# The second MLP's output product by seven block products, with its x operands stored in DRAM

## Chip, cores and metric

The kernel runs on one core of a Trainium2 chip. The metric is the device time of the program in microseconds (us), median of the runs shown. All matrix work is on TensorE (PE); VectorE (DVE), ScalarE (ACT) and GpSimd (POOL) prepare operands and drain results; every DMA is issued from the queue of SyncE (SP).

## What is computed

With 4 batches of 576 tokens, 8 heads of 64, width DM = 512 and hidden width DF = 1536:

```python
x = attention(q, k, v)                       # windowed, 2304 x 512
xn = x / rms(x) * rms_g                      # first MLP
x = (silu(xn @ w_gate) * (xn @ w_val)) @ w_out
gate = 1 / (1 + exp(-(x @ w_gate2)))         # second MLP, the part that changes
out = (gate * (x @ w_val2)) @ w_out2         # 2304x512 . 512x1536, then 2304x1536 . 1536x512
```

float32 accuracy is kept by splitting each operand into a rounded part (hi, type fp32r) and the rest (lo = value - hi); a product is three matmuls: hi·hi, hi·lo, lo·hi. `split` (L464) makes the two parts: a cast, on ACT or DVE, then a subtraction, on POOL or DVE.

## The kernel before

The work goes through in three stages. Attention and the norm come first, mixed with the first MLP's first pass (passes p = 0 and 1 hold six blocks of 128 hidden columns each, `mlp_step`, matmuls at L1033). The second MLP follows in three passes (p = ONE..LAST) that hold NF = 4 hidden blocks each; a pass goes over the four batches b, forward and backward in turn, and each batch is two units u of two hidden blocks.

`unit` (L1197) computes gate and value for one batch and two hidden blocks. The 2x2 block product (two halves of the width DM, two halves of the 576 tokens) is done by seven block products for eight, with left operands ("11", "12", "22" and the sums S1..S4, made by `weight_blocks`, L535) and right operands ("11", "21", "22" and the differences T1..T4, made by `x_blocks`, L970). One product is six matmuls of 128x128 by 128x288 (L1218). Results collect in three PSUM banks X, Y, Z; X is read out between products by `snap` (ACT, L1228) and `plus` (DVE, L1234), and `finish` applies the gate (ACT tanh, L1244; DVE, L1250) and splits the result into h.

`x_blocks` runs for ten of the twelve (pass, batch) pairs: it loads two tiles `xq` of the first MLP's result from DRAM, makes four differences of 128x576 (L986, or L989 on POOL) and seven splits of 128x576 into the tiles `xo`, `wst`, `xo2`.

The output product is the plain one: `y_group` (L1058, matmuls at L1070) multiplies one hidden block by one block of 128 output columns for 288 tokens, three matmuls of 128x128 by 128x288, and adds up over the four hidden blocks in one of four PSUM banks. Per pass, batch and token half that is 4 x 4 x 3 = 48 matmuls. `late` hands the 32 groups of a batch to the next batch's two units, where they are set between the unit's products; the last batch's are run at the end. `y_evac` (L1136) adds a finished bank to the sums of the passes before (`pt`, L1148; in the first pass a copy, L1141 on DVE or L1143 on ACT), which are kept in DRAM between passes (`o_part`). In the last pass `out_blocks` (L1160) turns a block on DVE and stores it, and `out_rows` (L1175) turns the last token chunk on PE. `weight_late` and `weight_out` prepare the output weights `wo`: twelve splits of 128x512.

The order of instructions on every engine is fixed when the program is built. Each operation is added with its engines, a cost, what it reads and writes and a due time; `Line.emit` is a list scheduler that repeatedly takes, for each engine, the operation that can start first by its own estimates (the due time breaks ties and lets urgent ones pass), and emits it. Tiles come from rings of a fixed number of buffers, so an operation that needs a buffer is placed only when its former user is planned to be done. The numbers in `PARAMS` are due times, penalties for an operation's other engine (`w_hi`, `x_lo`, ...), and release times (`rel2`, `span2`: when the second MLP's weights may be decoded by `words`, L417, and stored by `weight_ahead`, L511). Engines then run their queues in that order, each waiting on semaphores.

## Time and profile before

| | us |
|---|---|
| median of 3 runs | 1047.61 |
| the runs | 1047.01, 1047.61, 1050.1 |
| span of the profiled execution | 1042.3 |
| median less span | 5.3 |

| engine | busy us | share of the span |
|---|---|---|
| PE | 994.6 | 95% |
| DVE | 672.1 | 64% |
| POOL | 539.3 | 52% |
| ACT | 455.0 | 44% |

The profile is of one execution; its span runs from the first to the last instruction, and what lies around the span (5.3 us against the median) is not in it. A matmul is booked with its full latency and overlaps the next, so the pace of PE is read from the distance between starts, not from the booked time. A group's mean time on DVE and POOL contains what the two engines cost each other; the minimum and the median of a view by tile show it without that.

### The profile page before, as it was taken

The numbers are of one execution on the slowest core, as the hardware profiler recorded it, in microseconds if no ns is written. First come the engines' busy times: TensorE is split into PE (matmuls) and PEld (weight loads), VectorE is DVE, ScalarE is ACT, GpSimd is POOL, SyncE is SP. The second block draws the span as 40 slices with busy tenths as digits, with TensorE's granted clock in tenths as the row PEclk, the third lists the DMA queues.
The fourth block names the chain that finished last, engine by engine and source line by source line (L and its number), as shares of the span: only waits on it lengthen the run. The fifth ranks groups of instructions, "written<-read, shape, count | busy, mean of one in ns | idle before, by whom it ended". The sixth has DMA issues, their size and how long they took to land.

```text
span 1042.3 us, 19960 instructions
## 1 busy us (share of the span) xinstructions
PE 994.6 (95%) x7222; PEld 961.2 (92%) x7222; DVE 672.1 (64%) x1431; ACT 455.0 (44%) x1243; POOL 539.3 (52%) x691
## 2 busy tenths in 40 slices
PE   5889789999999999999999999999999999999997
PEld 4667678889999999999999989999999999999996
DVE  4688875676674478778777567456655577465633
ACT  3767646665332442222222454445543355443331
POOL 3467674554453663112114777558655398445510
PEclk9879879999999999999999999999999999999998
DMA  8957646673647565867782331213241433244334
GB/s 182 163 138 179 145 119 169 129 210 111 213 134 260 192 217 183 302 227 233 237 270 94 112 106 56 92 42 128 70 152 50 137 113 129 80 110 119 61 77 92
DMA packets 192978, 152.04 MB, mean 146 GB/s; under 512 B 135760, under 2 KB 164432, under 8 KB 192880
## 3 DMA queue, kind: packets, MB, share of 16 engines
q1 hardware_dynamic: 192880, 150.77, 49.6%
q8 instruction: 57, 0.93, 0.4%
q14 instruction: 41, 0.34, 0.1%
HBM read 103.55 MB, written 47.19 MB: 145 GB/s over the span
## 4 chain that ended last, share of the span: by engine, by line
PE 81%; DVE 7%; POOL 4%; DMA 3%; issue 2%; ACT 2%; SPq 1%; DVEq 0%; POOLq 0%; ACTq 0%
PE y L1070 25%; PE v L1033 14%; PE g L1033 14%; PE att L1218 9%; PE g L1218 6%; PE v L1218 6%; PE att L758 2%; PE att L814 1%; PE att L802 1%; POOL w L470 1%; DMA xo<-in_k_dram 1%; DVE S L545 1%; POOL xo L470 1%; SPq L596 1%; DVE t L1250 1%
## 5 line engine op out<-in xcount | busy, mean ns | idle before, releaser
L1070 PE MATMUL y<-h,wo 128*128 128x288 f32 (+1 forms) x2016 | 367.8, 312 | 0.5 <-POOL h L470 0.5
L1070 PEld LDWEIGHTS y<-h,wo 128*128 128x128 f32 x2016 | 318.6, 188 | 2.0 <-POOL h L470 0.8
L470 POOL TENSOR_TENSOR h<-t,h 128x288 fp32r<-128x288 f32 (+1 forms) x165 | 164.7, 1001 | 279.5 <-ACT h L466 267.4
L1033 PE MATMUL g<-xo,w 128*128 128x384 f32 x864 | 171.1, 346 | 4.8 <-POOL w L470 3.5
L1033 PE MATMUL v<-xo,w 128*128 128x384 f32 x864 | 165.5, 339 | 0.5 <-POOL w L470 0.5
L1033 PEld LDWEIGHTS g<-xo,w 128*128 128x128 f32 x864 | 154.7, 194 | 8.6 <-POOL w L470 4.4
L1033 PEld LDWEIGHTS v<-xo,w 128*128 128x128 f32 x864 | 152.1, 190 | 2.0 <-POOL w L470 1.3
L466 ACT CAST h<-t 128x288 fp32r<-128x288 f32 (+1 forms) x168 | 78.1, 468 | 142.4 <-DVE t L1051 81.0
L1218 PE MATMUL att<-xo,w 128*128 128x288 f32 x576 | 92.2, 295 | 1.3 <-DVE t L1234 1.3
L1045 ACT ACTIVATE t<-g 128x384 f32<-128x384 f32 x72 | 35.4, 492 | 131.2 <-PE g L1033 131.0
L1234 DVE TENSOR_TENSOR t<-t,att 128x288 f32<-128x288 f32 x96 | 43.2, 450 | 71.4 <-PE att L1218 68.0
L1047 DVE SCALAR_TENSOR_TENSOR t<-t,g 128x384 f32<-128x384 f32 x72 | 39.7, 551 | 67.0 <-ACT t L1045 66.9
L1218 PEld LDWEIGHTS att<-xo,w 128*128 128x128 f32 x576 | 81.5, 188 | 1.5 <-DVE t L1234 1.5
L788 POOL TENSOR_SCALAR pr<-pr,rs 128x96 f32<-128x96 f32 x135 | 55.7, 428 | 51.4 <-DVE rs L783 39.0
L470 POOL TENSOR_TENSOR xo<-xq,xo 128x576 fp32r<-128x576 f32 x38 | 58.8, 1555 | 27.5 <-ACT xo L466 22.9
L1218 PE MATMUL v<-xo,w 128*128 128x288 f32 x396 | 63.5, 296 | 1.5 <-DVE t L1234 1.3
L1218 PE MATMUL g<-xo,w 128*128 128x288 f32 x396 | 63.2, 295 | 0.0
L1051 DVE TENSOR_TENSOR t<-t,v 128x384 f32<-128x384 f32 x72 | 39.8, 553 | 34.8 <-PE v L1033 33.8
L456 DVE SCALAR_TENSOR_TENSOR wz<-wst,wz 128x512 int32<-128x512 int32 x72 | 60.9, 848 | 1.4
L459 DVE SCALAR_TENSOR_TENSOR wz<-wst,wz 128x512 int32<-128x512 int32 x72 | 61.0, 850 | 1.1
L453 DVE SCALAR_TENSOR_TENSOR wz<-wst,wz 128x512 int32<-128x512 int32 x72 | 57.1, 793 | 1.6
L1218 PEld LDWEIGHTS v<-xo,w 128*128 128x128 f32 x396 | 55.9, 188 | 2.2 <-DVE t L1234 1.8
(169 smaller groups left out, 1556.2 us busy)
## 6 DMA issues: line engine op xcount, KB each, us to landing
z<-wz SPq DMA_DIRECT2D x54, 256.0 KB
wst<-in_moe_w_gate_dram SPq DMA_DIRECT2D x24, 512.0 KB
wst<-in_moe_w_val_dram SPq DMA_DIRECT2D x24, 512.0 KB
wst<-in_moe_w_out_dram SPq DMA_DIRECT2D x24, 512.0 KB
xq<-y SPq DMA_DIRECT2D x20, 576.0 KB
x<-xo SPq DMA_DIRECT2D x12, 768.0 KB
xo<-x SPq DMA_DIRECT2D x12, 768.0 KB
z<-z SPq DMA_DIRECT2D x36, 256.0 KB
```

Source lines behind the costliest of these rows:

```text
L453: add("DVE", Shared(0.68), lambda: nc.vector.scalar_tensor_tensor(out=z.t, in0=top(), scalar=3, in1=z.t, op0=ALU.logical_shift_left, op1=A ...
L456: add("DVE", Shared(0.68), lambda: nc.vector.scalar_tensor_tensor(out=z.t, in0=top(), scalar=-0x40000000, in1=z.t, op0=ALU.bitwise_and, op ...
L459: add("DVE", Shared(0.68), lambda: nc.vector.scalar_tensor_tensor(out=z.t, in0=low(), scalar=29, in1=z.t, op0=ALU.logical_shift_right, op1 ...
L466: add("ACT", act(n), lambda: nc.scalar.copy(out=hi(), in_=src()), reads=reads, writes=[key] + [order] * bool(order), tiles=tiles + [dst], ...
L470: add("PL", pool(n), lambda: nc.gpsimd.tensor_tensor(out=lo(), in0=src(), in1=hi().bitcast(F32), op=ALU.subtract), reads=reads, writes=[ke ...
L788: add("PL", Shared(0.33), lambda u=u: nc.gpsimd.tensor_scalar(out=pr.t[:, u], in0=pr.t[:, u], scalar1=rs.t[:, u:u + 1], scalar2=1.0, op0=A ...
L1033: nc.tensor.matmul(out=bank.t, lhsT=w[:, l, cols], rhs=x[:, r, j], start=kk == 0 and n == 0, stop=kk == KD - 1 and n == 2)
L1047: add("DVE", dve(T1), lambda: nc.vector.scalar_tensor_tensor(out=t.t, in0=t.t, scalar=1.0, in1=gb.t, op0=ALU.add, op1=ALU.mult), writes=[k ...
L1051: add("DVE", dve(T1), lambda: nc.vector.tensor_tensor(out=t.t, in0=t.t, in1=vb.t, op=ALU.mult), reads=[("bank", p, c, f, 1)], writes=[key] ...
L1070: nc.tensor.matmul(out=yb.t, lhsT=w.t[:, l, s], rhs=h.t[:, r], start=n == 0 and j == 0, stop=n == nf - 1 and j == 2)
L1218: nc.tensor.matmul(out=bank.t, lhsT=l.t[:, a, cols], rhs=r.t[:, d, j], start=first and j == 0 and m == 0, stop=j == 1 and m == 2, skip_gro ...
L1234: add("DVE", dve(T), lambda: nc.vector.tensor_tensor(out=t.t, in0=t.t, in1=bank.t, op=ALU.add), reads=[(key, uk)], writes=[ck[name]], tile ...
```

## The change

The output product of the second MLP is done by seven block products for eight as well. The 2x2 blocks are two hidden blocks of a unit's pair against two halves of 256 output columns (e), and the two token halves. `unit` no longer splits four h tiles; it makes four differences of the gated blocks (`combos`) and seven splits `hop`. `weight_blocks_out` makes seven left operands `wy` out of two `z` tiles, with four sums. `y_products` runs, per pass and batch, 2 x 7 products of six matmuls (two units, three matmuls each), in three of the four PSUM banks y0..y3, and after each product `sum_part` adds the bank to one or two sums; the products are placed in the next batch's units, from slot `y_from` in steps of `y_step` (a slot is one product of the unit).

`x_build` replaces `x_blocks`: it runs once per batch, for batches 0 and 1 during the first MLP's second pass and for 2 and 3 in the second MLP's first pass, and stores each operand in DRAM (`xop_scr`). `x_ops` loads the seven operands where they are used otherwise. The order of the seven products is changed (ORDER, RIGHT, the unit's steps), rings are resized, `out_rows` and `out_blocks` work by halves of the columns, and PARAMS is changed.

```diff
-    "margin": 272.425, "wait": 0.781, "w_sq": 2.027, "w_hi": 0.518, "w_lo": 0.708, "x_hi": 0.345, "x_lo": 0.688,
-    "h_hi": 0.72, "h_lo": 0.667, "qk": 0.226, "norm": 3.767, "pts": 4.555, "o": 0.012, "snap": 38.426, "h_ahead": 56.759, "h2_ahead": 33.839, "evac": 150.0, "holds": (6, 6), "norm_act": 0.994, "slack": 0.0, "share_v": 0.45, "share_p": 0.35, "cold": 1.7, "low": 0.27, "high": 0.38, "recip": 0.43, "rel1": 171.35, "span1": 76.226, "rel2": 360.0, "span2": 192.706, "ys": 1.364,
...
+    "margin": 272.425, "wait": 0.781, "w_sq": 2.027, "w_hi": 0.389, "w_lo": 1.94, "x_hi": 0.358,
+    "x_lo": 0.048, "h_hi": 1.944, "h_lo": 0.349, "qk": 0.226, "norm": 3.767, "pts": 4.555,
+    "o": 0.012, "snap": 53.824, "h_ahead": 56.759, "h2_ahead": 11.517, "evac": 7.152,
+    "rel2": 16.017, "span2": -0.378, "ys": 11.771, "ts": 0.198, "cross": 0.08, "same": 0.064,
+    "exp_cost": 0.56, "s_cost": 0.75, "o_cost": 0.6, "t_cost": 0.38, "pt_lead": 6.997,
+    "x_lead": 91.83, "wy_due": -0.712, "y_from": 5.542, "y_step": 1.029, "xb_due": 1.637,
+    "y_last": 0.244, "xb_last": 13.017,
...
-    W_HOMES = ("sb", "w", NW), ("bp", "w2", 4)
-    O_HOMES = (("sb", "wo", NO),)
+    W_HOMES = ("sb", "w", NW), ("bp", "w2", 2)
+    O_HOMES = ("sb", "wo", NO), ("bp", "wo2", 1)
...
+    def weight_blocks_out(p, u, due):
+        z = [weight_load(p, f + k, 2, due - 6) for k in range(2)]
...
+        for name in ORDER:
+            if name == "S1":
+                combine("S1", blk(1, 0), blk(1, 1), ALU.add, zk, z)
...
+            split(w, lambda w=w: w.t[:, u, 0], lambda w=w: w.t[:, u, 1], src, KW,
+                  ("wy", p, u, name), reads, [], tiles, due, "w", "o order")
...
-    RIGHT = ("11", "21", "T2", "T1", "T3", "22", "T4")
+    RIGHT = ("11", "T1", "T2", "22", "T3", "21", "T4")
...
+    def combos(blk, key, n, due):
...
+            add("DVE", dves(n), lambda: nc.vector.tensor_tensor(
+                out=dst(), in0=a(), in1=c(), op=ALU.subtract), reads=reads, writes=writes,
+                tiles=tiles, due=due,
+                other=("ts", "PL", pool(n), lambda: nc.gpsimd.tensor_tensor(
+                    out=dst(), in0=a(), in1=c(), op=ALU.subtract)))
...
+            if name == "T1":
+                combine(at(0, 0), at(0, 1), at(0, 0), [key(0, 1)], [key(0, 0)],
+                        [tile_(0, 1), tile_(0, 0)])
+            elif name == "T2":
+                combine(at(0, 0), at(1, 1), at(0, 0), [key(1, 1)], [key(0, 0)],
+                        [tile_(0, 0), tile_(1, 1)])
...
+    def x_build(b, due):
...
+            dma(lambda o=o, i=i: nc.sync.dma_start(
+                out=xop_scr[7 * b + i].bitcast(F32), in_=o.t.bitcast(F32)), X_BYTES,
+                reads=[key], writes=[("xst", b, name)], tiles=[o], due=due + 2)
+    def x_ops(p, b, dues):
+        for i, name in enumerate(RIGHT):
+            o = xop[p, b, name] = x_tile(p)
...
+                out=o.t.bitcast(F32), in_=xop_scr[7 * b + i].bitcast(F32)), X_BYTES,
...
+    AHEAD = 2
+    X_LATER = ["xq"] * 2 + ["xo"] * 3 + ["xs"] + ["wst"] * 3 + ["xo"]
...
+    def sum_part(p, b, n, e, h, bank, key, first, last, due):
+        if first and p == ONE:
+            two = "ACT", act(T), lambda: nc.scalar.mul(out=t.t[:, e, h], in_=bank.t, mul=0.5)
...
+        else:
+            add("DVE", dve(T), lambda: nc.vector.scalar_tensor_tensor(
+                out=t.t[:, e, h], in0=bank.t, scalar=0.5, in1=t.t[:, e, h], op0=ALU.mult,
+                op1=ALU.add), reads=[key], writes=[sk], tiles=[bank, t], due=due)
...
+    def y_products(p, b):
+        steps = (("X", (("11", 1, 0),)), ("Y", (("22", 1, 0),)), ("X", (("12", 1, 0),)),
+                 ("Y", (("12", 0, 1),)), ("X", (("22", 0, 1),)), ("Z", (("11", 0, 1),)),
+                 ("X", (("21", 1, 1),)))
...
+                    for u in range(NF // 2):
+                        for m, (a, d) in enumerate(((0, 0), (0, 1), (1, 0))):
+                            nc.tensor.matmul(out=bank.t, lhsT=w.t[:, u, a, n], rhs=hs[u].t[:, d],
...
+        return [one(n, i) for n in range(KD // 2) for i in range(7)]
...
             steps = (("X", lambda: snap("11", X, "X")),
+                     ("Y", lambda: snap("22", Y, "Y")),
+                     ("X", lambda: snap("12", X, "X")),
+                     ("Y", lambda: (plus("12", Y, "Y"), finish("12"))),
+                     ("X", lambda: (plus("22", X, "X"), finish("22"))),
                      ("Z", lambda: (plus("11", Z, "Z"), finish("11"))),
...
+        for name, src, k, tile_ in combos(blk, lambda k, h: ("t", f"{k + 1}{h + 1}", hk),
+                                          T, due):
+            o = hop[p, b, u, name] = one_of(H_HOMES, [P, 2, T], F32R)
+            split(o, lambda o=o: o.t[:, 0], lambda o=o: o.t[:, 1], src, T,
+                  ("hop", p, b, u, name), [k], [], [tile_], due, "h")
...
+                step = PARAMS["y_last" if (p, n) == (LAST, B - 2) else "y_step"]
+                extra = [(PARAMS["y_from"] + step * i, fn)
+                         for i, fn in enumerate([fn for _, fn in extra] + y_products(p, b))]
+        for _, fn in extra:
+            at += fn(at)
```

## Rows read from the trace of the kernel before

**Rows 1.** The page: busy time and share of the span of each engine.

```profile
PE 994.6 (95%) x7222; PEld 961.2 (92%) x7222; DVE 672.1 (64%) x1431; ACT 455.0 (44%) x1243; POOL 539.3 (52%) x691
```

**Rows 2.** Windows by stage: length, busy time of PE, PEld, DVE, ACT, POOL; clock, DMA.

```profile
606.30:1019.00 412.70, 407.91 (x3070) 405.87 (x3069) 245.39 (x431) 179.72 (x446) 247.22 (x233) 1.00 0.32 96
1019.00:1032.40 13.40, 13.40 (x104) 13.40 (x103) 6.05 (x16) 0.77 (x2) 1.99 (x3) 1.00 0.51 101
1032.40:1042.30 9.90, 2.36 (x14) 1.23 (x13) 1.85 (x5) 1.65 (x3) 0.00 (x0) 0.68 0.47 104
0.00:300.00 300.00, 265.37 (x2279) 235.88 (x2280) 209.29 (x661) 172.49 (x584) 167.05 (x329) 0.94 0.65 158
300.00:606.30 306.30, 305.58 (x1764) 304.79 (x1763) 209.48 (x322) 100.42 (x209) 122.99 (x128) 1.00 0.61 204
```

**Rows 3.** Waits of PE in the second MLP: total us, times, longest.

```profile
PE att L1218 <- ACT t L1228: 2.0, 3, 1.4
```

**Rows 4.** Timeline of PE in the last batch: start, us, line, count.

```profile
1004.71 0.96 PE L1218 MATMUL g<-wst,w 128*128 128x288 f32 x6
1005.51 0.56 PE L1070 MATMUL y<-h,wo 128*128 128x288 f32 x3
1005.90 0.96 PE L1218 MATMUL att<-wst,w 128*128 128x288 f32 x6
...
1018.98 13.68 PE L1070 MATMUL y<-h,wo 128*128 128x288 f32 x102
```

**Rows 5.** Groups by form on DVE, POOL, ACT, 606 to 1020: count, busy us, mean ns.

```profile
L1250 DVE SCALAR_TENSOR_TENSOR t<-t,t 128x288 f32<-128x288 f32 x71 | 54.7, 771 | 1.1
...
L1148 DVE SCALAR_TENSOR_TENSOR pt<-y,pt 128x288 f32<-128x288 f32 x56 | 24.0, 446 | 0.4 <-PE y L1070 0.4
...
L470 POOL TENSOR_TENSOR h<-t,h 128x288 fp32r<-128x288 f32 x91 | 80.0, 884 | 93.2 <-ACT h L466 81.2 <-issue 9.2 <-POOL wst L470 0.9
...
L470 POOL TENSOR_TENSOR wo<-z,wo 128x512 fp32r<-128x512 f32 x7 | 9.3, 1325 | 11.8 <-ACT wo L466 11.8
...
L466 ACT CAST h<-t 128x288 fp32r<-128x288 f32 x94 | 40.3, 433 | 56.7 <-DVE t L1250 54.7 <-PE y L1070 1.3
```

**Rows 6.** By tile (S, xq, t), from 606 on: duration ns min/median/max.

```profile
L470 POOL TENSOR_TENSOR w<-S,w x32: 727/738/1239, 610.9 to 886.0; 128x256 fp32r<-128x256 f32 x32
...
L545 DVE TENSOR_TENSOR S<-z x13: 414/953/1649, 625.2 to 882.2; 128x256 f32<-128x256 f32 x13
...
L470 POOL TENSOR_TENSOR xo<-xq,xo x36: 1418/1540/1873, 604.4 to 983.4; 128x576 fp32r<-128x576 f32 x36
L986 DVE TENSOR_TENSOR xq<-xq x20: 744/759/1358, 620.5 to 964.6; 128x576 f32<-128x576 f32 x20
...
L470 POOL TENSOR_TENSOR h<-t,h x91: 797/808/1317, 616.0 to 1018.6; 128x288 fp32r<-128x288 f32 x91
...
L1250 DVE SCALAR_TENSOR_TENSOR t<-t,t x71: 430/698/1682, 614.6 to 1017.6; 128x288 f32<-128x288 f32 x71
```

**Rows 7.** Timeline 595 to 622: two equal DVE operations; a load and its user.

```profile
596.81 1.25 DVE L545 TENSOR_TENSOR S<-z 128x256 f32<-128x256 f32 x1 [0.73 <-POOL w L470]
...
598.14 0.43 DVE L545 TENSOR_TENSOR S<-S,z 128x256 f32<-128x256 f32 x1
...
610.92 0.80 SPq L976 DMA_DIRECT2D xq<-y  x2
...
615.32 0.46 DVE L468 CAST xo<-xq 128x576 fp32r<-128x576 f32 x1 [0.27 <-DMA xq<-y]
```

**Rows 8.** Waits of the SP queue, whole span: total us, times, longest.

```profile
SPq L1156 <- DVE pt L1141: 62.7, 8, 16.2
```

**Rows 9.** Timeline of the end: start, us, what, [idle before and its releaser].

```profile
1035.51 0.48 DVE L1165 STREAM_TRANSPOSE ob<-pt 128x288 f32<-128x288 f32 x1 [1.74 <-DMA out_dram<-ob]
1036.27 1.36 SPq L1194 DMA_DIRECT2D out_dram<-z  x3
1037.72 1.95 SPq L1171 DMA_DIRECT2D out_dram<-ob  x4
```

More of the change, by code (lines that the diff above doesn't have):

```diff
@@ L429, in load @@
                                   in_=w[f * P:f * P + P, :])
-        dma(load, 524e3, writes=["w order", ("wst", key)], tiles=[st], due=load_due,
+        dma(load, 524e3, writes=["wst order", ("wst", key)], tiles=[st], due=load_due,
             release=release)
@@ L1121, in part_load @@
             return
-        if p < ONE:
-            t = parts[p, c] = new("sb", "pt", [P, KD, T1], F32, 2)
-            dma(lambda: nc.sync.dma_start(out=t.t, in_=y_part[c]), 786e3,
-                reads=[("part", p - 1, c), ("bank", p, c, FIRST[p], 0)],
-                writes=[("sum", p, c, m) for m in range(KD)] + ["pt order"], tiles=[t], due=due)
-            return
-        t = parts[p, c] = new("sb", "pt", [P, KD, T], F32, 2)
+        t = parts[p, c] = new("sb", "pt", [P, KD, T1], F32, 2)
@@ L1132, in part_load @@
                 ["pt order"], tiles=[t], due=due)
     LAST = ONE + TWO - 1
[L1136 to L1146 removed]
+    LAST_B = B - 1 if TWO % 2 else 0
@@ new lines, in sum_part @@
+    def sum_part(p, b, n, e, h, bank, key, first, last, due):
+        t = parts[p, b, n]
+        sk = ("sum", p, b, n, e, h)
+        if first and p == ONE:
+            one = "DVE", dve2(T), lambda: nc.vector.tensor_scalar(
+                out=t.t[:, e, h], in0=bank.t, scalar1=0.5, scalar2=None, op0=ALU.mult)
+            two = "ACT", act(T), lambda: nc.scalar.mul(out=t.t[:, e, h], in_=bank.t, mul=0.5)
+            add(*two, reads=[key], writes=[sk, "pt order"], tiles=[bank, t], due=due,
+                other=("ys", *one))
```

345 lines of the change are left out of this document (201 added, 144 removed).

## The prediction

> **What bounds the kernel now.** The page comes first: PE is busy 95% of the span, DVE 64%, POOL 52% [rows 1]. Then the windows by stage, because the share is an average: ahead of 300 us PE is busy 265.37 of 300, so the first stage loses 34.6 us to waits; from 300 to 606.3 it is busy 305.58 of 306.30; in the second MLP (606.3 to 1019) 407.91 of 412.70, which leaves 4.8 us of waits; then 13.40 us of output products with nothing beside them and an end of 9.90 us [rows 2]. Whatever takes matmuls out of the second MLP is therefore paid at full price, unless new waits take its place. The waits of PE there are few and short, on ACT's and DVE's reading of the banks, 2.0 us for the largest [rows 3]. PE's pace is read from starts: six matmuls take 0.80 us and three take 0.39, nine in 1.19, or 0.132 us each, at a granted clock of 1.00, the 2.4 GHz level [rows 2, 4].
>
> **Matmuls.** Before, the output product takes 3 passes x 8 chunks x 4 hidden blocks x 4 column blocks x 3 = 1152 matmuls. After, it takes 12 (pass, batch) pairs x 2 x 7 products x 6 = 1008, of the same shape. 144 fewer, at 0.132 us: -19.0 us. `unit` keeps its 2016. This is the one term that is certain, since the products run in an order written down and PE has no idle time for them to fall into.
>
> **POOL, DVE and ACT in the second MLP.** The seven products need more preparation for h and less for x.
> - h: 168 splits for 96 and 96 new differences of 128x288. 72 more POOL subtractions at 0.884 us: +63.6; 72 more ACT casts at 0.433: +31 [rows 5]. The trace has no difference of 128x288; the nearest operation of DVE with two SBUF inputs of that size is the gate's, 0.43 us at least and 0.771 in the mean [rows 5, 6]: +41 to +74 on DVE.
> - x: 4 builds for 10, two of them ahead of 606. In the second MLP 14 splits are left of 63 and 8 differences of 36: 49 x 1.54 = -75 us on POOL, 28 x 0.76 = -21 on DVE [rows 6], and casts on both other engines that I leave uncounted.
> - output weights: 42 splits of 128x256 for 12 of 128x512, and 24 sums. POOL 42 x 0.738 - 12 x 1.325 = +15; DVE 24 x 0.414 to 0.953 = +10 to +23 [rows 5, 6].
> - sums: 168 bank reads for 96; 32 go to ACT, 136 to DVE for 80: 56 x 0.446 = +25 on DVE [rows 5].
>
> POOL comes to 247 + 4 = 251, DVE to 300 to 346, ACT to about 220 us, of a stage of some 395 us. None of them is the bound, so at face value all of it is hidden under PE. What it costs is slack. DVE and POOL disturb each other: a sum of 128x256 took 1.25 us beside POOL and the next one 0.43 [rows 7], and the gate's operation 0.43 to 1.682 [rows 6]. So I add up, at the shortest durations, DVE's operations with two SBUF inputs and POOL's subtractions. Before: 96 x 0.43 + 48 x 0.414 + 40 x 0.744 + 96 x 0.797 + 84 x 0.727 + 12 x 1.325 + 70 x 1.418 = 344 of the 426 us from 606.3 to 1032.4. After: 192 x 0.43 + 72 x 0.414 + 16 x 0.744 + 168 x 0.797 + 126 x 0.727 + 28 x 1.418 = 390, less 26 for the two builds made earlier, 364 of 407. The free share goes from 19% to 11%. PE waited 4.8 us with 19%; I let the waits grow as the free share shrinks, 4.8 x 19/11 = 8.3 to 8.7, and take +3.9 us. Bounds: -4.8 (all waits go, since the x build no longer sits in front of each batch) and the slow rival below.
>
> The Trainium skill (SBUF — State Buffer, section Who interferes with whom) says that a VectorE instruction with two SBUF inputs and a GpSimd one that reads SBUF exclude each other for the whole instruction. The trace agrees: 1.25 us is 0.43 plus about one POOL subtraction of 0.8. By that rule the 364 of 407 is a real load of one shared resource, and speaks for the first rival.
>
> **What is moved.** The two early builds (14 splits, 8 differences, four `xq` loads, 14 stores) fall into the last stretch of the first MLP; from 300 to 606 POOL is free for 183 and ACT for 206 of 306 us and PE runs nearly without waits [rows 2]. I cost them at nothing: PE does not need these operands before the second MLP, and POOL's free time hides them. With that cover gone, each h of the first MLP could stand behind one x subtraction, 1.54 us [rows 6]. Decoding the second MLP's weights may begin at 16 us of the plan for 360; it stays in order behind the first MLP's weights on its ring, and that ring's release times end at 247 us of the plan (rel1 + span1), so it fills DVE from about there on. Together with the changed penalties it also reorders the first stage. There the trace shows nothing of the new order: bounds of a tenth of the 34.6 us that PE loses there, -3.5 and +3.5, and 0 as my value.
>
> On the SP queue 56 loads and 28 stores of 576 KB are added and 12 `xq` loads dropped. A pair of such loads landed 4.4 us after issue (610.92 to 615.32) [rows 7], 2.2 each. Seven are 15.4 us, the sums' two loads and two stores 8.8, so 24 us of a batch's 34. Ten tiles serve seven operands, so three loads run ahead and the rest are issued when the former batch's last unit lets a tile go, about ten products, at least 8 us, before use. Hidden. An x load waits on PE for its tile, and behind it on SP stand the sums' loads and stores and the weights' loads; ahead of it can stand a store of sums that waits on DVE, 62.7 us in 8 waits, up to 16.2 [rows 8].
>
> **The end.** Now the last batch's 13.4 us of products start on h of the first unit, so the last unit's splits are covered. After, every product needs both units. From the last unit's end: "11" is read one product earlier, so 0.45 + 0.43 to 0.77 + 0.43 + 0.80 to 0.88 - 0.8 = 1.3 to 1.7 us until the first product. T1 and T2 each follow by difference, cast and subtraction, 1.66 to 2.08: 3.0 to 3.8, 4.6 to 5.9. The other four come one POOL subtraction apart, T4 at 7.8 to 9.4. The first half ends at 8.6 to 10.2, the second 5.6 later, 14.2 to 15.8 against 13.4: +1.6 (0.8 to 2.4). Behind it, now, a transpose on DVE waits 1.74 us for an earlier store, and its four stores, 1.95 us, are issued last [rows 9]. After, block stores belong to the first half and go out under the second. Up to 3.7 us of the 9.9 go; I take 3.0, bounds 0 and 3.7. Together -1.4, bounds -2.9 and +2.4.
>
> **Sum.** Against the profiled execution: 1042.3 - 19.0 + 3.9 - 1.4 + 0 = 1025.8 of span, and with the 5.3 us by which the median of the runs exceeds the span 1031.1. I forecast 1031.
>
> **Rivals.** Slower: the splits of h come too late at each batch boundary. Before, h of a batch had most of a unit until its use; now the first output product stands six unit products (4.8 us) behind the unit's end and the others 1.62 us apart (1.029 slots of 0.8 and one product), so T2 is due at 8.0. By the durations used for the end it is ready at 4.6 to 5.9. At the longest durations of the trace (1.682 on DVE, 1.317 on POOL) [rows 6] the first takes 0.45 + 1.68 + 0.43 + 1.32 - 0.8 = 3.1 and two links of 3.43 make 9.9: 1.9 us late, in twelve batches 23 us, and 1054 us. It decides from (19.0 + 1.4 - 3.9) / 12 = 1.4 us per batch. For it speaks the free share of 11%, and that with every new pass the weights' splits stand in the same POOL queue; against it that POOL's median is 0.808, and that DVE's spread shows single collisions, not rows of them. 15%.
>
> No difference: x loads come late. Eight batches load all their operands; one load's landing (2.2 us) lost at each is 17.6 us, and 1048.7. For it: the SP waits [rows 8]; against: three tiles of reserve, a DMA share of 0.32 in this stage [rows 2]. 10%.
>
> Faster still: the waits at the x builds vanish, the end takes its best bound and the first stage gains: 1047.6 - 19.0 - 4.8 - 2.9 = 1020.9, down to 1017. For it: a subtraction of x holds POOL for 1.54 us, twice as long as one of h [rows 6], and most of these go; against: the free share. 15%.
>
> That the products are not fewer can't be: the loops count them. My own case holds 60%, between 1024 and 1041.
>
> **Numbers.** About 0.3% (3 us) is what a measurement tells from no change. Faster: 0.60 + 0.15 + a little of the second rival, 0.77; same 0.08; slower 0.15. The range reaches from the third rival to the second, 1020 to 1049, and leaves out most of the first.
>
> **What would show it.** Right: PE's pace in the second MLP still 0.132 us, 3024 matmuls in it, the stage from its first product to its last near 412 us (426 - 19 + 3.9 + 1.6), PE waits of 6 to 12 us in it; a wait of 1 to 4 us between the last unit and its first output product; an end after PE's last product under 8 us; the first product of the second MLP still near 606. Wrong: PE waits on POOL or ACT h (the `hop` tiles) of over a microsecond after each batch; PE waits on a DMA into `xq`, `xo` or `wst`; a first product of the second MLP off by more than 4 us, which would say that the reordered first stage carries the difference.

## The result: slower, with three stretches off

| | runs | median us | from | to |
|---|---|---|---|---|
| before | 4 | 1048.72 | 1047.01 | 1050.1 |
| after | 4 | 1061.45 | 1057.64 | 1063.01 |

The ratio is 1.0125 [1.0099, 1.0152]; forecast were 1031 and a range of 1020 to 1049. The profiled execution of after took 1063.01 us with a span of 1061.2: 1.8 us lie around the span, and 1.7 to 1.9 in every execution of after and of before that lists both. So the execution of before that the prediction read (span 1042.3) took about 1044.1, and was one of its quicker ones.

The engines of after (busy time, share, instructions), which answer to [rows 1], and below them its windows by stage, which answer to [rows 2] (stretch, length, busy time and count of PE, PEld, DVE, ACT, POOL, granted clock, DMA share, GB/s):

```profile
PE 995.7 (94%) x7078; PEld 953.3 (90%) x7078; DVE 728.1 (69%) x1559; ACT 483.5 (46%) x1338; POOL 553.4 (52%) x757
```

The windows:

```profile
0.00:300.00 300.00, 261.49 (x2222) 231.59 (x2222) 208.97 (x667) 170.27 (x576) 163.31 (x324) 0.91 0.65 159
300.00:624.80 324.80, 318.33 (x1823) 315.95 (x1822) 222.24 (x331) 107.21 (x222) 135.43 (x137) 0.99 0.68 236
624.80:1037.00 412.20, 399.31 (x2944) 391.40 (x2943) 285.05 (x540) 201.65 (x531) 249.66 (x291) 1.00 0.49 167
1037.00:1055.70 18.70, 15.68 (x88) 13.80 (x88) 11.34 (x23) 3.38 (x8) 4.97 (x7) 0.82 0.17 29
1055.70:1061.20 5.50, 0.88 (x7) 0.50 (x5) 0.46 (x1) 0.95 (x2) 0.00 (x0) 0.90 0.46 121
```

The units' window has 2944 records of matmuls for 3070 [rows 2], yet is as long as before. It begins 18 us later, and in it PE idles 12.9 us (412.20 - 399.31) for 4.8. Divided at starts of matmuls (first product of the second MLP, last unit's last product, last output product):

| stretch, us | before | after | difference | forecast |
|---|---|---|---|---|
| until the second MLP's first product | 606.5 | 624.8 | +18.3 | 0 |
| its units | 412.3 | 411.4 | -0.9 | -12.7 |
| output products after the last unit | 13.5 | 19.2 | +5.7 | +1.6 |
| rest | 9.9 | 5.8 | -4.1 | -3.0 |

(-12.7 is 126 of the 144 matmuls, -16.6, and +3.9 of waits; the other 18 lie in the tail, the output products after the last unit, which are 102 matmuls before and 84 after.) PE's waits in the units of after (waiting line, releaser, total us, times, longest), against [rows 3]:

```profile
PE g L1361 <- POOL xo L477: 3.0, 2, 1.5
PE v L1361 <- ACT t L1371: 2.2, 4, 1.5
PE att L1361 <- ACT t L1371: 2.1, 4, 0.7
PE g L1361 <- DVE t L1377: 1.7, 2, 1.3
PE v L1361 <- DVE t L1377: 1.0, 2, 0.6
PE y L1280 <- POOL h L477: 0.8, 3, 0.3
PE g L1361 <- DMA xo<-xs: 0.4, 1, 0.4
```

Most are reads of a bank (`t` of L1371 and L1377, 7.3 of 12.8 us), as before, only more of them. The first row is new: two waits for the x builds that were left in the first pass, at the first products of batches 2 and 3. 0.8 us are waits for h, the first rival's place, and 0.8 (this and a second row) for x loads, the second's. Short gaps are in no wait row, so below I also count **gaps**: how far two consecutive starts of PE lie apart beyond 0.1325 us, where that is over 0.06. In the units they add up to 7.2 us before and 21.5 after.

### The profile page after: what moved, and what is told of

It is laid out like the page before. It is cut to its first block, busy times and chain, and to the rows that moved or that the text cites. A ratio compares the mean times of both kernels' runs of the same rounds, so it can differ in the third digit from the quotient of the medians.

```text
span 1061.2 us, 20091 instructions
## 1 busy us (share of the span) xinstructions
PE 995.7 (94%) x7078; PEld 953.3 (90%) x7078; DVE 728.1 (69%) x1559; ACT 483.5 (46%) x1338; POOL 553.4 (52%) x757
## 5 line engine op out<-in xcount | busy, mean ns | idle before, releaser
L477 POOL TENSOR_TENSOR h<-t,h 128x288 fp32r<-128x288 f32 (+1 forms) x219 | 206.7, 955 | 303.7 <-ACT h L473 285.2
L473 ACT CAST h<-t 128x288 fp32r<-128x288 f32 (+1 forms) x240 | 108.6, 457 | 175.9 <-DVE t L1142 93.5
L1159 PE MATMUL y<-h,wo 128*128 128x384 f32 x864 | 171.3, 342 | 0.8 <-POOL h L477 0.4
L1280 PE MATMUL y<-h,wo 128*128 128x288 f32 x1008 | 162.1, 299 | 3.9 <-POOL h L477 1.8
L1124 PEld LDWEIGHTS v<-xo,w 128*128 128x128 f32 x864 | 151.7, 190 | 6.2 <-DVE t L1142 5.3
L1239 DVE SCALAR_TENSOR_TENSOR pt<-y,pt 128x288 f32<-128x288 f32 x136 | 61.4, 452 | 61.9 <-PE y L1280 53.1
L1136 ACT ACTIVATE t<-g 128x384 f32<-128x384 f32 x72 | 35.4, 492 | 121.3 <-PE g L1124 121.2
L841 POOL TENSOR_SCALAR pr<-pr,rs 128x96 f32<-128x96 f32 x139 | 60.1, 449 | 39.7 <-DVE rs L836 18.8
L1377 DVE TENSOR_TENSOR t<-t,att 128x288 f32<-128x288 f32 x96 | 43.0, 448 | 39.3 <-PE att L1361 36.6
L457 DVE TENSOR_SCALAR wz<-wz 128x512 f32<-128x512 f32 x72 | 44.9, 623 | 32.1 <-ACT wz L451 31.8
L463 DVE SCALAR_TENSOR_TENSOR wz<-wst,wz 128x512 int32<-128x512 int32 x72 | 64.1, 890 | 1.4
L451 ACT ACTIVATE wz<-wst 128x512 f32<-128x512 f32 x71 | 47.5, 669 | 28.2 <-DMA wst<-in_moe_w_gate_dram 11.2
L466 DVE SCALAR_TENSOR_TENSOR wz<-wst,wz 128x512 int32<-128x512 int32 x72 | 59.2, 824 | 1.4
L1026 DVE TENSOR_TENSOR t<-t,t 128x288 f32<-128x288 f32 x62 | 49.3, 796 | 13.9 <-POOL h L477 13.5
L828 ACT ACTIVATE pr<-pr,nmx 128x96 f32<-128x96 f32 x144 | 52.4, 367 | 11.6 <-DVE nmx L822 11.3
```

Source lines behind the costliest of these rows:

```text
L463: add("DVE", Shared(0.68), lambda: nc.vector.scalar_tensor_tensor(out=z.t, in0=top(), scalar=-0x40000000, in1=z.t, op0=ALU.bitwise_and, op ...
L466: add("DVE", Shared(0.68), lambda: nc.vector.scalar_tensor_tensor(out=z.t, in0=low(), scalar=29, in1=z.t, op0=ALU.logical_shift_right, op1 ...
L473: add("ACT", act(n), lambda: nc.scalar.copy(out=hi(), in_=src()), reads=reads, writes=[key] + [order] * bool(order), tiles=tiles + [dst], ...
L477: add("PL", pool(n), lambda: nc.gpsimd.tensor_tensor(out=lo(), in0=src(), in1=hi().bitcast(F32), op=ALU.subtract), reads=reads, writes=[ke ...
L841: add("PL", Shared(0.33), lambda u=u: nc.gpsimd.tensor_scalar(out=pr.t[:, u], in0=pr.t[:, u], scalar1=rs.t[:, u:u + 1], scalar2=1.0, op0=A ...
L1026: add("DVE", dves(n), lambda: nc.vector.tensor_tensor(out=dst(), in0=a(), in1=c(), op=ALU.subtract), reads=reads, writes=writes, tiles=til ...
```

## Experiments on the first stage

Each time stands against the kernel before run beside it on the same chip; where kernels of different chips are compared in us, it is by their distances from that. The diffs show of a long line only the numbers that change. Split penalties (`w_hi`, ..., `ts`) and release times (`rel2`, `span2`) were set back, each alone and both; and both were put into the kernel before.

**e1_release**, times of release as before:

```diff
-    "rel2": 16.017, "span2": -0.378,
+    "rel2": 360.0, "span2": 192.706,
```

> The changed kernel with the release of the second MLP's weight decode as before (rel2 360, span2 192.7), all else changed. In the trace of the changed kernel the second MLP begins 18.3 us later than before, in jumps: 5.0 by the first step of the first MLP, 3.8 by step 13, 1.3 at step 25, 5.6 at step 35 (PE waits 2.94 us for the gate on DVE, which stands behind four decode operations, and the clock falls), 2.1 at step 62. Theory R (the earlier decode fills DVE ahead of the gate): the jumps at 13, 25 and 35 go, the second MLP begins near 614, the time is 1061 - 10 = 1050 +- 3. Theory P (the changed split penalties reorder the first stage): the start stays at 620 to 626, the time within 3 us of the changed kernel. Theory S (any reordering of the first stage moves it by several us): a start anywhere between 606 and 626.

**e2_penalties**:

```diff
-    "w_hi": 0.389, "w_lo": 1.94, "x_hi": 0.358, "x_lo": 0.048, "h_hi": 1.944, "h_lo": 0.349, "ys": 11.771, "ts": 0.198,
+    "w_hi": 0.518, "w_lo": 0.708, "x_hi": 0.345, "x_lo": 0.688, "h_hi": 0.72, "h_lo": 0.667, "ys": 1.364, "ts": 0.0,
```

> The changed kernel with the penalties of splits, bank copies and differences as before (w_hi, w_lo, x_hi, x_lo, h_hi, h_lo, ys, ts), the release as changed. Theory R: within 3 us of the changed kernel, about 1061, the wait at step 35 still there. Theory P: the first stage's 8.6 us come back, 1052 +- 3. In the second MLP, where the trace shows 21.5 us of excess distance between matmul starts against 7.2 before, the penalties of before send more bank copies to DVE: if the excess is DVE's, it grows by some us.

**e3_both**: both edits.

> The changed kernel with the release and the penalties both as before: what stays is the block product of the output, the stored x operands, the rings and the due times of the second MLP. Theories R and P together: the second MLP begins within 4 us of 606, the time is 1044 to 1048 (before, less 19.0 for the matmuls, plus 14 for the waits in the units and 2 for the end). If the early x builds are what disturbs the first MLP instead, the start stays above 616 and the time above 1055.

**e4_before_new**: the kernel before with both edits reversed, and no block product.

> The kernel before with the changed release and penalties, and nothing else of the change. Theories R and P: its second MLP begins some 18 us later, near 624, and the time is 1060 to 1068. If the delay comes from the x builds or the output product, this kernel takes 1046 to 1052.

In the table "PE idle until then" is the time until the second MLP begins in which PE had nothing to do, and the last two columns are the length of the units and the gaps in them, in us. A matmul at a lower clock counts as a gap, too: the granted clock in the units was 1.00 before, after and in e4, 0.99 in e1 and e2, and 0.97 in e3 (of later runs 0.97 in e6, e8, e11 and e14, 0.96 in e12, 0.99 in e17, else 1.00).

| | median us | ratio to before | second MLP begins | PE idle until then | units | gaps |
|---|---|---|---|---|---|---|
| after | 1061.45 | 1.0125 [1.0099, 1.0152] | 624.8 | 45.0 | 411.4 | 21.5 |
| e1 (old release) | 1067.05 | 1.0205 [1.0173, 1.0236] | 620.0 | 40.3 | 422.3 | 32.1 |
| e2 (old penalties) | 1064.06 | 1.0173 [1.0142, 1.0203] | 613.8 | 41.6 | 420.2 | 29.9 |
| e3 (both old) | 1068.8 | 1.0216 [1.0183, 1.0249] | 611.8 | 35.5 | 431.1 | 41.0 |
| before | 1044.84 | 1 | 606.5 | 35.4 | 412.3 | 7.2 |
| e4 (before, both new) | 1056.63 | 1.011 [1.0081, 1.0138] | 619.0 | 43.3 | 413.0 | 7.8 |

PE idle is length less busy PE in the two windows up to the begin; e4's, with its units in the third row:

```profile
0.00:300.00 300.00, 261.93 (x2245) 231.89 (x2245) 209.42 (x669) 170.60 (x577) 164.06 (x324) 0.90 0.67 161
300.00:619.00 319.00, 313.82 (x1805) 312.48 (x1801) 210.13 (x318) 101.64 (x212) 130.06 (x134) 0.99 0.57 193
619.00:1032.90 413.90, 408.25 (x3074) 406.36 (x3073) 238.62 (x437) 185.29 (x454) 222.03 (x219) 1.00 0.31 96
```

These numbers of PARAMS alone, with not one product fewer, cost the kernel before 11.8 us, nearly all ahead of 619. In the changed kernel the idle time ahead of the second MLP goes 45.0, 40.3, 41.6, 35.5 as release, penalties and both go back: the release is worth 4.7 or 6.1 us, the penalties 3.4 or 4.8, and with both gone nothing is left over before's 35.4. The time from the first MLP's first product to the second's holds, besides waits, the matmuls behind them that ran at a lower clock. It is 541.9 us before, 555.2 after, 551.7 in e1, 547.3 in e2, 543.2 in e3 and 551.4 in e4. By it the release is worth 3.5 or 4.1 us and the penalties 7.9 or 8.5, and with both gone 1.3 us over before are left. So the two early x builds, which e3 still makes there, are hidden, as forecast. But e3 is the slowest: its units take 431.1 us. For 9.5 us of idle time early the two settings save 19.7 us in the units.

The release's place can be seen in after. Four decode operations of second-MLP weights (L466 to L463) and, behind them, the first MLP's gate (L1142) stand in DVE's one queue; PE's product waits for the gate:

```profile
376.42 1.11 DVE L466 SCALAR_TENSOR_TENSOR wz<-wst,wz 128x512 int32<-128x512 int32 x1
376.55 2.25 PE L1124 MATMUL g<-xo,w 128*128 128x384 f32 x12
...
377.45 0.95 DVE L457 TENSOR_SCALAR wz<-wz 128x512 f32<-128x512 f32 x1
...
378.44 1.64 DVE L460 SCALAR_TENSOR_TENSOR wz<-wst,wz 128x512 int32<-128x512 int32 x1
...
380.12 1.10 DVE L463 SCALAR_TENSOR_TENSOR wz<-wst,wz 128x512 int32<-128x512 int32 x1
381.13 0.54 DVE L1142 TENSOR_TENSOR t<-t,v 128x384 f32<-128x384 f32 x1
...
381.73 4.21 PE L1124 MATMUL v<-xo,w 128*128 128x384 f32 x12 [2.94 <-DVE t L1142]
```

With the old release (e1, e3) no wait of PE is left at this place; with the old penalties alone (e2) three shorter ones, of 1.3, 0.5 and 0.8 us, stand around it. What the early release buys is seen in e1, whose output weights come too late; PE's timeline there:

```profile
659.68 0.85 PE L1280 MATMUL y<-h,wo 128*128 128x288 f32 x2 [6.23 <-ACT wo L473]
```

Three runs sought the gain in the units without the loss ahead of them. **e5_staged** gives splits of the norm and of the first MLP the old penalties, and leaves the rest of after:

```diff
+    "w0_hi": 0.518, "w0_lo": 0.708, "x0_hi": 0.345, "x0_lo": 0.688, "h0_hi": 0.72, "h0_lo": 0.667, "ys0": 1.364,
-              [], [t], s + 3.7 - p * PARAMS["h_ahead"], "h")
+              [], [t], s + 3.7 - p * PARAMS["h_ahead"], "h0")
...
```

> The changed kernel, but splits and bank copies of the first MLP and the norm take the penalties of before, those of the second MLP the changed ones; release as changed. With the penalties of before throughout (e2_penalties) the second MLP began at 613.8 instead of 624.8, but its units took 420.2 us instead of 411.4. If the two stages want different penalties: begin at 612 to 616, units 410 to 413, time 1050 to 1055. If penalties of the first stage work on the second MLP only through the order they leave behind (which weights are ready when), the units take 416 or more and the time stays above 1057.

**e10_release_split** and **e14_release_steps** are e5 with other releases of weight n (e10: 16 for the first twelve, then late; e14:)

```diff
-            weight_ahead(p, f, i, t - 8, t, PARAMS["rel2"] + PARAMS["span2"] * n / len(todo))
+            weight_ahead(p, f, i, t - 8, t, (362.0 + 5.3 * n if n < 6 else 394.0 + 3.0 * (n - 6)))
```

> e5_staged with the release of the weight decode changed: the first pass's twelve weights at 16 as in the change, the other 24 from 395 of the plan in steps of 5. In e5_staged steps 32 to 37 of the first MLP take 35.5 us against 31.8 before (decode of the second MLP's weights and splits of the first MLP's second pass meet on DVE and POOL). Theory R: these come back, 3 to 4 us, begin at 611 to 613, 1048 to 1049, if no weight comes late for the second MLP. Against: in e1_release the late decode cost 6.5 us in one wait for the output weights; if the order of the units is hurt again, 1052 to 1058.

> e5_staged with the weight decode released as before for its first six weights (362 of the plan, steps of 5.3) and faster behind (394, steps of 3). If the decode ahead of 394 is what crowds DVE in steps 32 to 37: 31.8 us there instead of 35.5, begin at 611 to 613; units as in e5_staged (411 to 413) and a time of 1047 to 1049, since the last weight is decoded about as early. If the units lose it again by weights that come late, as in e1_release: 1052 or more.

e5 took 1051.68 us, ratio 1.0058 [1.0034, 1.0082]; its second MLP begins at 615.8, PE is idle 38.0 us until then, and the units take 411.5. So old penalties ahead of the second MLP take back half of what the change lost (+6.2 us over before for +12.7) and cost the units nothing. e10 took 1053.74 us, 1.0063 [1.0044, 1.0083], and nothing moved (begin 616.6), so the weights that crowd DVE can only be among the first twelve, which e10 leaves early. e14, which releases those later too, took 1061.34, 1.014 [1.0124, 1.0157]: it is idle 36.4 us until its begin at 608.6, but its units take 427.2 with gaps of 37.0. What the first stage gains there the units lose twice over.

## Experiments on the units

e5's units still take 411.5 us, although 16.7 us of matmuls are gone. Three things were candidates: x operands, differences of h, and the places of the output products. Those are now 14 of six matmuls per batch for 32 of three, so more unit products have no output product within the two products before them: 1074 matmuls after, 162 before. I call these matmuls uncovered: the bank that such a product is to fill must be read in the time of one product.

**e9_before_stored**: before, with x stored in the first of the three passes and loaded in the others. **e13_stored_bunched**: e9 and the edit of e7.

```diff
...
-                    x_blocks(p, b, at - 26)
+                    (x_blocks if p == ONE else x_ops)(p, b, at - 26)
```

> The kernel before with the second half of the change alone: x operands are built for the four batches of the second MLP's first pass as before, each stored in DRAM (28 stores of 576 KB), and the two later passes load them (42 loads) for the six builds dropped; the output product stays the plain one, order and rings stay. Theory: the storing helps a little or nothing, since PE waits only 3.3 us in the batches behind the first: 1043 to 1047 against 1045.5 before. Rival: the loads stand in SP's queue behind waiting stores and come late: 1048 or more, with PE waits on DMA into xo, wst or xo2.

> e9_before_stored (the kernel before with x operands loaded in the two later passes; POOL busy 176 us in the units for 247) with the output groups bunched as in e7_before_bunched. Bunching cost 10.3 us there, with 16.3 us of excess. Theory C (cover alone decides): again 9 to 12 us over the kernel before, 1055 to 1058. Theory L (missing cover costs only where POOL and DVE are loaded): excess under 8 us and a time of 1046 to 1050; the first pass, where x is still built, keeps its 5 to 9 us.

**e7_before_bunched**: before, with a batch's output products in the first half of their slots, so that the second half is uncovered; no work is added.

```diff
-                while done < total * n // 14:
+                while done < min(total, total * n // 7):
```

> The kernel before with its plain output groups set two by two behind the first seven of each unit's fourteen products, none behind the other seven; nothing else. No matmul, split or difference is added. Theory C: matmuls of the units without an output group in the two products before them go from 162 to about 950, and at 11 to 24 ns each (changed kernel, kernel before) the time rises by 9 to 19 us, to 1055 to 1064. Theory L: DVE and POOL have the same work, the time stays within 3 us of the kernel before.

**e15_bunched**: e5 with the output products closer together.

```diff
-    "y_from": 5.542, "y_step": 1.029,
+    "y_from": 8.0, "y_step": 0.55,
```

> e5_staged with the output products closer together and later: first at slot 8, in steps of 0.55, so all 14 stand within slots 8 to 16 of 28 and twelve slots more than a quarter behind none. No work is added. Theory C: unit matmuls without cover rise from 1074 to about 1450, their excess from 12 to some 16 to 20 us, time +4 to +8, 1056 to 1060. Theories D and L: same load and chain, units within 3 us; later first products even give h more time, and the 3.2 us of excess at output products fall.

**e16_no_differences**: e5 without the four differences of h; each split reads one of the plain gated blocks, so the output isn't the reference's.

```diff
-        for name, src, k, tile_ in combos(blk, lambda k, h: ("t", f"{k + 1}{h + 1}", hk),
-                                          T, due):
...
+        for name, (k0, h0) in [(name, homes[name]) for name in RIGHT]:
+            src, k, tile_ = blk(k0, h0)[0], key(k0, h0), blk(k0, h0)[1]
```

> e5_staged without the four differences of h in each unit: the seven splits read the plain gated blocks, so the output is not the reference's. 96 DVE (or POOL) operations of 128x288 go; all casts, subtractions, products and bank reads stay. Theory D (the chain difference, cast, subtraction holds up the queues in front of the bank reads): excess in the units from 21.6 to 8 to 12 us, units 398 to 403, the wait at the end 3 to 5 us shorter, time 1034 to 1041. Theory C alone: excess stays at 18 or more, and only the end gains: 1046 to 1050.

| | median us | ratio to before | begin | units | tail | gaps in the units | uncovered matmuls: gaps |
|---|---|---|---|---|---|---|---|
| before | | 1 | 606.5 | 412.3 | 13.5 | 7.2 | 162: 3.9 |
| e7 | 1055.8 | 1.0095 [1.007, 1.012] | 612.5 | 423.7 | 12.7 | 16.3 | 948: 16.3 |
| e9 | 1046.03 | 0.9998 [0.9983, 1.0014] | 610.4 | 411.8 | 13.5 | 6.5 | 162: 1.4 |
| e13 | 1046.11 | 0.9999 [0.9988, 1.001] | 609.5 | 414.1 | 12.7 | 6.9 | 948: 5.6 |
| after | 1061.45 | 1.0125 [1.0099, 1.0152] | 624.8 | 411.4 | 19.2 | 21.5 | 1074: 12.3 |
| e5 | 1051.68 | 1.0058 [1.0034, 1.0082] | 615.8 | 411.5 | 18.6 | 21.6 | 12.0 |
| e15 | 1065.41 | 1.0188 [1.0166, 1.021] | 613.7 | 423.4 | 19.4 | 32.3 | 1368: 29.9 |
| e16 | 1040.99 | 0.9944 [0.9923, 0.9964] | 615.2 | 401.8 | 15.4 | 11.8 | 9.5 |

The windows of the units, with the columns as above. e7:

```profile
612.50:1037.00 424.50, 414.42 (x3080) 409.19 (x3079) 249.11 (x428) 183.19 (x453) 252.07 (x236) 1.00 0.30 95
```

e13, with the same places and a smaller load:

```profile
609.50:1024.50 415.00, 411.83 (x3080) 408.96 (x3079) 201.65 (x390) 169.09 (x428) 179.15 (x191) 1.00 0.52 176
```

e5:

```profile
615.80:1028.10 412.30, 398.51 (x2945) 391.31 (x2943) 284.57 (x538) 202.04 (x533) 250.15 (x292) 1.00 0.49 169
```

e16, the units and the tail:

```profile
615.20:1017.80 402.60, 396.44 (x2944) 391.14 (x2942) 250.45 (x489) 195.84 (x518) 224.52 (x265) 1.00 0.51 173
1017.80:1032.70 14.90, 12.50 (x88) 11.73 (x88) 9.73 (x20) 2.62 (x7) 3.05 (x4) 1.00 0.20 33
```

e9 takes 70 us from POOL and 47 from DVE [rows 2] and gains nothing: nobody waited for the x builds. e7 shows that uncovered products cost by themselves, 10.3 us in its time and 11.4 in its units. e13 has the same places with DVE at 202 us for 249 and POOL at 179 for 252, and its time is e9's: its units are 2.4 us longer than e9's, and its tail and end give that back. So in these kernels a missing cover costs 11.4 us with x built and 2.4 with x loaded; it is dear where DVE and POOL are loaded. e15 says the first of the changed kernel: +12.5 us over e5 by places alone.

And e16 has e5's places but not its differences, with DVE at 250 for 285 and POOL at 225 for 250: its units are 9.7 us and its tail 3.2 shorter, and the time is 11.9 us less (-5.7 against before for +6.2). The gaps of its units fall by 9.8 us, the largest single term behind the forecast's +3.9: 2.5 at uncovered products, 4.3 at covered ones and 3.1 at output products. The edit takes away the differences' load and their places in the queues at once, so it doesn't tell these two apart.

How a difference delays PE is in after's DVE and PE timelines (start, us, line, tiles, count, idle before and its releaser). The bank reads of `att` and `g` (L1377) stand behind three differences (L1026) on DVE:

```profile
654.45 3.17 DVE L1026 TENSOR_TENSOR t<-t,t 128x288 f32<-128x288 f32 x3
657.54 0.45 DVE L1377 TENSOR_TENSOR t<-t,att 128x288 f32<-128x288 f32 x1
657.90 0.45 DVE L1377 TENSOR_TENSOR t<-t,g 128x288 f32<-128x288 f32 x1
```

PE's next product fills `g` and starts when the second of these reads has ended:

```profile
658.40 1.06 PE L1361 MATMUL g<-xo,w 128*128 128x288 f32 x6 [1.26 <-DVE t L1377]
```

Three differences took 3.17 us, and PE's next product waited 1.26 us for the reads behind them. Of the 92 differences in the units 58 are in this row (11 more on DVE have other names, and 23 are on POOL), by duration (minimum, median, maximum in ns):

```profile
L1026 DVE TENSOR_TENSOR t<-t,t x58: 445/864/1689, 638.7 to 1032.1; 128x288 f32<-128x288 f32 x58
```

The h tiles' casts and subtractions:

```profile
L473 ACT CAST h<-t x162: 415/434/444, 636.5 to 1036.0; 128x288 fp32r<-128x288 f32 x162
L477 POOL TENSOR_TENSOR h<-t,h x148: 797/813/1332, 637.1 to 1036.5; 128x288 fp32r<-128x288 f32 x148
```

The median difference takes twice its least time, so the median, too, holds what the two engines cost each other, and only the minimum is free of it; ACT's casts stay within 7%. That agrees with the Trainium skill (SBUF — State Buffer, section Who interferes with whom): a VectorE operation with two SBUF inputs and a GpSimd one that reads SBUF shut each other out for a whole instruction, and ScalarE waits for nobody. The rule's size was in the prediction; what stands in line behind such an operation was not.

Four runs were misses. **e6_spread** (after, `y_step` 1.42) and **e8_mix** (e5, `y_step` 1.25, release 200 and 120) put output products further apart, for fewer uncovered ones:

> The changed kernel with the output products spread wider among the unit's products: y_step 1.42 for 1.029, so 14 of them reach to slot 24 of 28 instead of 19. In the changed kernel 12.3 us of the 21.5 us of excess lie at unit products with no output product in the two products before them (1074 matmuls; before: 162 with 3.9 us). Theory C (an output product between two unit products covers the reading of the bank X): these matmuls fall to some 650, the excess there to about 7.5, the time by 3 to 6 us, to 1055 to 1058. Theory L (DVE and POOL are simply busier, wherever the products stand): the excess stays at 20 or more, the time within 2 us of the changed kernel. A third way: later output products give up their h tiles later, and the next unit's splits wait: time rises.

> The changed kernel with three things at once: penalties by stage as in e5_staged, output products at y_step 1.25, and the weight decode released at 200 us of the plan over 120 us (between 16 and 360). If theories P, R and C each hold and add: begin of the second MLP at 609 to 613, units 405 to 409, tail as before the experiments (19 + 6), time 1043 to 1049. If the order left behind counts instead, anything up to 1062.

e6 took 1088.95 us, 1.0405 [1.0383, 1.0428]; uncovered matmuls fell to 714, but gaps rose to 49.3, 31.9 of them at covered ones. PE's waits in its units:

```profile
PE v L1361 <- ACT t L1371: 16.0, 7, 5.2
PE v L1361 <- DVE t L1377: 5.8, 6, 2.3
```

PE waits up to 5.2 us for one read by ACT. The expectation had named a third way, in which h tiles are given up later and splits wait for them. The trace doesn't show that at the longest wait (until 906.46): in ACT's queue ahead of that read ran four casts of weights, three gate operations and two casts of h that waited 0.16 and 0.47 us for differences on DVE, and none that waited for a tile. Why the order put them there stays open. e8 took 1074.43 us, 1.0265 [1.024, 1.0289], with units of 432.7; it changed three things at once and tells no more.

**e11_ahead3** (e5, `AHEAD = 3`) and **e12_release_ahead** (e11 with e10's release) build x a batch earlier:

> e5_staged with three batches' x operands built during the first MLP instead of two (AHEAD 3), so only one build is left in the second MLP's first pass. In e5_staged PE waits 2.9 us for POOL's subtractions of x in two places of that pass, and 12 of the 21.6 us of excess lie in its four batches. Theory L2 (the units' waits come where POOL and DVE have the builds and the weights' splits to do while no output product covers the banks): excess of that pass falls by 3 to 6 us, time 1046 to 1049. Theory C alone (cover decides, load does not): excess unchanged, 1051 to 1053. If the third build disturbs the first MLP's last steps: the begin moves up by what the units gain.

> e10_release_split and e11_ahead3 together. If both help and add: 1043 to 1047, level with the kernel before or just under it. If the third build and the later decode meet in the last steps of the first MLP: above both.

Both lose one wait of over 30 us to the load into the single `xs` tile, and take 1087.62 and 1087.5 us; e11's row, with the columns of the waits:

```profile
PE g L1363 <- DMA xs<-xs: 31.5, 1, 31.5
```

Its gaps elsewhere are 23.0 us, for e5's 21.6, so moving a build ahead gains the units nothing either.

## Both ways in one kernel

**e17_two_passes** is e5 with the plain product in the first of the three passes, which there has no differences of h and no sums of output weights, and with before's release; **e18_two_passes_early** has after's release.

```diff
-    "rel2": 16.017, "span2": -0.378,
+    "rel2": 360.0, "span2": 192.706,
...
+    def y_plain(p, c, f, m, due):
```

> e5_staged with the plain output product in the second MLP's first pass (four splits of h per unit, no differences, output groups spread over all 28 slots) and the block product in the two later passes; release of the weight decode as before (360 over 193). 96 matmuls fewer than before, 12.7 us. From rows: first-pass excess as in the kernel before (some 5 us), the two later passes as in e5_staged (8 us against 2.5), the end +1.3, begin as before. Theory (the block product pays where POOL and DVE are free): 1046.5 - 12.7 + 5.5 + 1.3 = 1040.6, 1038 to 1044. Rival: weights of the later passes come late or the turn from plain to block product stalls: 1046 or more.

> The same with the changed release (16): steps 32 to 37 of the first MLP take 3.7 us more, as in e5_staged, and the weights are ready earlier. If nothing in the second MLP waits for weights in e17_two_passes: 3 to 4 us slower than that, 1043 to 1046. If it does: level or faster.

e17 took 1054.91 us, 1.0079 [1.0058, 1.0099], with its begin at 611.1 and units of 414.9; 6.6 us of its 18.8 us of gaps lie in one stretch of 33 us at the third pass's beginning. e18 took 1052.28, 1.0049 [1.0036, 1.0062], with its begin at 614.0, units of 409.4 and gaps of 13.3. No kernel that computes the reference beats the one before; e9 and e13 are level with it.

## Why the prediction was wrong

**The account.** The forecast missed by 30.4 us: first stage +18.3, units +11.8, tail +4.1, end -1.1. 2.4 more is a slip: eighteen of the 144 matmuls lie in the tail, which was compared as a whole (13.4 us before are 102 matmuls, not the last batch's 96), so they were counted twice. And -5.1 is what I put around the span (5.3), where after's median stands 0.25 over its span: those 5.3 were 1.8 and a lucky, short draw of before.

**"0 as my value" for the reordered first stage** failed first. 9.6 of the 18.3 us are waits of PE, 45.0 for 35.4, outside the bounds of ±3.5; e1 to e3 split them into release and penalties, and e4 shows them without the rest of the change. The other 8.7 are matmuls that were booked longer, at a granted clock of 0.91 in the first 300 us for 0.94 [rows 2]. PE's first product of the first MLP, before and after, divides the stage further:

```profile
64.57 0.69 PE L1033 MATMUL g<-xo,w 128*128 128x384 f32 x1
69.61 0.69 PE L1124 MATMUL g<-xo,w 128*128 128x384 f32 x1 [0.25 <-ACT xo L473]
```

5.0 of the 18.3 us lie ahead of it, and no run shows them to be the change's: e7, e9 and e13, with before's order of that stage, had this product at 67.5 to 70.5 us. From there to the second MLP's first product before and these three took 541.9 to 542.2 us and after 555.2. So +13.3 is the change's: 9.3 of waits (23.9 for 14.6), and 4.0 of longer matmuls at a granted clock of 0.97 for 0.98, as behind the wait of 2.94 us. The prediction had named this as a sign of being wrong, a first product off by more than 4 us. The bound was a tenth of PE's idle time in the stage. But after 300 us PE had 0.7 us of waits and the other engines were 33 to 68% busy [rows 2]; an order that had no waits could only get worse. "Fills DVE from about there on" stood in the text and was not priced: four decode operations ahead of one gate are the 2.94 us above.

**The units' waits** were mis-sized: +3.9 forecast, +14.3 by gaps. The bank reads were the right place for most of it and neither rival's; 3.0 us, the two waits for x builds, weren't in the forecast at all. But scaling 4.8 us by the free share took the load as the only cause. e7 and e13 show two factors, places and load, and the change raises both: over six times as many uncovered products, and 40 us more of DVE. The prediction never looked at what remains between two unit products when an output product goes. With the differences gone the gaps fall from 21.6 to 11.8 us and 11.9 us of time return (e16); of what is left, 9.5 lie at uncovered products. How that divides between places and DVE's order isn't shown.

**Matmuls, POOL, x loads** held: 126 fewer records in the units' window, POOL 249.7 us (251 forecast), DVE 285 and ACT 202 a little under theirs, and 0.8 us of PE for all loads. POOL's sum came out partly by luck: POOL also made 23 of the differences, which the forecast gave to DVE, and DVE 14 of the subtractions that it gave to POOL. The first rival, h late at the batch boundary, is refuted as a place by PE's 0.8 us for POOL's h (1.2 with DVE's), and the second by the rows of loads.

**The tail** was +5.7 for +1.6. PE's timeline there, against [rows 4]:

```profile
1036.36 0.55 PE L1280 MATMUL y<-h,wo 128*128 128x288 f32 x3
1038.14 0.40 PE L1280 MATMUL y<-h,wo 128*128 128x288 f32 x1 [1.23 <-ACT h L473]
1039.01 1.11 PE L1280 MATMUL y<-h,wo 128*128 128x288 f32 x5 [0.47 <-POOL h L477]
1040.55 0.61 PE L1280 MATMUL y<-h,wo 128*128 128x288 f32 x1 [0.43 <-ACT h L473]
1041.43 2.15 PE L1280 MATMUL y<-h,wo 128*128 128x288 f32 x6 [0.27 <-POOL h L477]
1043.84 2.53 PE L1280 MATMUL y<-h,wo 128*128 128x288 f32 x9 [0.27 <-POOL h L477]
```

The wait of 1 to 4 us before the first product was there (1.23). PE then waits for T1 and T2 (last at 1041.43 and 1043.84) and for no operand behind them. They come one link of 2.4 us after another, for my 1.66 to 2.08, since each link made two differences, two casts and two subtractions:

```profile
1038.99 1.54 DVE L1026 TENSOR_TENSOR t<-t,t 128x288 f32<-128x288 f32 x2 [1.00 <-POOL h L477]
1040.58 1.56 POOL L477 TENSOR_TENSOR h<-t,h 128x288 fp32r<-128x288 f32 x2 [0.86 <-ACT h L473]
1041.41 1.53 DVE L1026 TENSOR_TENSOR t<-t,t 128x288 f32<-128x288 f32 x2 [0.51 <-POOL h L477]
```

That is about 1.1 us of the 4.1. Two terms weren't in the sum. Six transposes of `out_rows` now stand ahead of the last twelve output products, 1.2 us (from 1052.65 to 1053.87). And PE's granted clock, 1.00 in before's tail [rows 2], was 0.82 here: it fell to its lower level, 1.2 GHz, at 1039.6 us, in the waits above, and rose again at 1046.4. e14 and e18 have the same output products there and kept a clock of 1.00; their tails took 17.4 us for 19.2, so the clock is some 1.8 us of it. e14's tail, with the columns of the windows:

```profile
1036.70:1053.50 16.80, 13.29 (x88) 11.87 (x88) 10.52 (x22) 3.25 (x8) 5.12 (x7) 1.00 0.18 30
```

e16's tail, 15.4 at 1.00, is 2.0 us shorter than these; the rest of its 3.2 to e5 is e5's clock, 0.91. Why the clock fell in some of these tails and not in others isn't shown. **The end** held: 5.5 us after PE's last product for under 8. The 1.1 us that it gained beyond the forecast are about what the transposes cost the tail.

## What to carry over

A change of planner numbers is a change like any other: price it by putting the numbers alone into the old kernel, and let a stage that runs without waits have only a loss as its bound. Work hidden under PE is priced by what stands behind it in an in-order queue, so ask of each bank read which operation is ahead of it, and how many products of PE cover it; a busy share, even one well under 100%, answers neither. Where a change puts waits into a stretch that had none, look at its granted clock too. Compare a predicted span with several executions before its distance from the median is taken for a constant.

## What the runs showed of the chip

The same instruction order on the engines up to the second MLP began it at 606.5, 609.5, 610.4 and 612.5 us, with idle time within 0.8 us; matmuls' booked time, 571.2 to 577.1 us, and granted clock, 0.94 to 0.88 over the first 300 us, made the difference. All of that spread arose ahead of the first MLP's first product (64.6 to 70.5 us); from there the four took 541.9 to 542.2 us. After PE's wait of 2.94 us, twelve matmuls of 128x384 took 4.21 us at a granted clock of 0.50, the 1.2 GHz level, where the twelve ahead of the wait took 2.25 at 1.00. In the tail the same 56 output matmuls took 7.81 us in e14 at 1.00 and 9.01 in e5, where the clock was at the lower level for part of them.
